# Sharing pooling and the gate's +1 with GpSimd, six gate groups by Sigmoid and a new instruction order in a pooled-attention and gated-convolution kernel

## The chip, the cores and the metric

The kernel runs on one core of a Trainium2 chip. The core has a matrix engine (TensorE, "PE" in the profile), three engines for element-wise work (VectorE "DVE", ScalarE "ACT", GpSimd "POOL") and SyncE "SP", which here only issues DMAs. Each engine executes its own instructions strictly in the order in which the program lists them, and waits on semaphores for the others. The metric is the device time of one execution in microseconds; the number quoted for a kernel is the median of its runs.

## The reference

Eight sequences of 576 rows are computed. For each, keys and values are averaged over groups of 8 rows, the 576 queries attend to the 72 pooled keys in 8 heads of 64, and the result goes through a feed-forward block in which a three-tap convolution along the sequence gates the hidden layer.

```python
k_p = k.reshape(B, H, Sp, pool, D).mean(axis=3)          # B, H, S, D = 8, 8, 576, 64; pool = 8
v_p = v.reshape(B, H, Sp, pool, D).mean(axis=3)
scores = scale * np.matmul(q, k_p.transpose(0, 1, 3, 2))
scores = scores - np.max(scores, axis=-1, keepdims=True)
attn = np.exp(scores)
attn = attn / (np.sum(attn, axis=-1, keepdims=True) + 1e-09)
x = np.matmul(attn, v_p)                                  # then heads side by side: (8, 576, 512)
h = np.maximum(x @ w_in, 0.0)                             # d_ff = 1024
conv_out = sum(conv_w[k] * hp[:, k:k + S, :] for k in range(3))   # hp is h, zero-padded by one row
gate = 1.0 / (1.0 + np.exp(-conv_out))
return h * gate @ w_out
```

Inputs and output are float32; inside, the matrices are bfloat16.

## The kernel before

**Groups and tiles.** The eight sequences ("b" 0 to 7) form four groups g of two. The 1152 rows of a group are cut into nine attention tiles t of 128 rows (ten in group 0, where the tile shared by both sequences is split in two of 64), 37 tiles in all. The rows of a sequence stand in an order in which row c of every run of nine lies together, so that a shift by one row is a shift by 64 columns with a wrap at the ends.

**Loads.** K of sequences 0 and 1, then K of the pairs (2,3), (4,5), (6,7), Q and V of each sequence, and the two weight matrices are loaded by DMAs that stand in POOL's queue (L272, L279, L290, L293, L300, L308). The load also converts to bfloat16. Buffers are few: one for a K pair (`kk`), four for Q (`qp`), three for V (`v`); a load into a buffer waits until the last use of what was in it.

**Pooling.** For sequences 0 and 1 K is pooled by a matmul with a pooling matrix (L391, L401). For the later pairs `pool_pair` (L424) adds halves in three steps on DVE, over all nine blocks at once: 128x2304, 128x1152 and 128x576 elements. V of every sequence is pooled by `prep_v`: three halving steps (L471, 128x1280, 128x640, 128x320) and a multiplication with a head mask into `vm` (L475, 128x960), all on DVE.

**Attention of a tile.** Scores (PE, L567 or L580), negated maximum (DVE, L593), the shift by it: either on DVE into a float32 tile `sd` (L605, 27 tiles) or as a matmul onto the scores (PE, L613, the ten tiles of group 0); exponential (ACT, L631); transposition of `e`, in groups 0 and 1 by PE and a copy (L642, L656), in groups 2 and 3 by a transposing DMA in SP's queue (L651); values with the sum of the exponentials in a 65th column (PE, L667); division (DVE, L680 and L682); transposition of `x`, again by PE and a copy (L699, L707) or by SP's DMA (L691).

**Feed-forward of a sequence.** For each of eight blocks fb of hidden columns 8 matmuls (L712) and a ReLU on ACT that writes 0.5·h (L721). Four blocks make a gate group f4, so there are 16 gate groups. In ten of them the convolution is done on PE with diagonal matrices (`ffn_conv`, L874), followed by Tanh on ACT (L899); half of the result comes out with its partition halves exchanged and goes to a side tile `tg`. In the other six (`TAPS`: (4,1), (5,0), (5,1), (6,0), (6,1), (7,0)) it is done by one ACT instruction (L847) and two DVE instructions (L849) for each block, then Tanh (L854). Since sigmoid(y) = (1 + tanh(y/2))/2, DVE then adds 1: L910 and two L912 (which undo the exchange) for a PE group, one L860 for a tap group. DVE multiplies by h (L920 or L861). The result is `gT`; 8 matmuls for each of 36 output tiles (L928), a copy (L939) and two stores (L951) follow. For sequences 4 to 7 POOL copies the wrapped ends of h (`ffn_wrap`, L796 and L797), which is POOL's only work beside loads and set-up.

**What sets the order.** Every piece of work is an `Op` in a `Graph`. The order of all instructions, the engine of those copies that DVE or ACT may do, and the buffer that each takes are written out in tables (`ORDER`, `FORMS`, `PLACES`); nothing is decided at run time. An entry -1 in `ORDER` stands for a filler matmul (L384) that computes nothing that is used.

Of the kernel before, what the change touches and what calls it, by code (L numbers as in the profile page):

```python
# [16 lines left out]

# [6 lines left out]
class Op:  # L24
    def __init__(self, engines, key, emit, uses, mode, land, count):
        self.engines, self.key, self.emit, self.mode, self.land, self.count = engines, key, emit, mode, land, count
        self.uses, self.next, self.left = list(uses), [], 0
        self.forms, self.like, self.dmas = None, None, 1
        self.ready, self.start, self.end, self.engine = 0.0, None, None, None
        for t in self.uses:  # L30
            t.users.append(self)


class Graph:

    SPARES = 150
    ATT = 90.28  # L40
    SPREAD = -122.92
    PREP_K = 135.88
    KPOOL = -99.86
    KTURN = 15.09
    PREP_Q = 1123.0
    PREP_V = 2242.18
    GATE = 390.96
    CONV = 199.25
    QCONV = -794.87
    OUT = 412.5  # L50
    LAST = 1107.48
    FIRST = 803.11
    V0 = -1430.11
    DW = -368.65
    X_DMA = 4
    APART = (0,)
    SIXTEEN = ()
    Q_DMA = (3,)
    WRAP = (4, 5, 6, 7)
    TAPS = ((4, 1), (5, 0), (5, 1), (6, 0), (6, 1), (7, 0))  # L60
    ACC = 2
    WRAPS = 2
    CROSS = ()
    BY_TILE = ()
    V_POOL = ()
    K_POOL = ()
    SHIFT_PE = ((0, 0), (0, 1), (0, 2), (0, 3), (0, 4), (0, 5), (0, 6), (0, 7), (0, 8), (0, 9))
    TURN_DMA = 2
    BANKS = 8
    ORDER = (  # L70
# [79 lines left out]
    def add(self, engines, key, emit, after=(), behind=(), uses=(), mode=None, land=None, count=10):  # L150
        o = Op(engines, key, emit, uses, mode, land, count)
        for a, started in [(x, False) for x in after] + [(x, True) for x in behind]:
            if a is not None:
                a.next.append((o, started))
                o.left += 1
# [22 lines left out]
def kernel(  # L178
# [13 lines left out]
    POOL = 8  # L192
# [59 lines left out]
    def buf(*key):  # L252
        return buffers[key[0]][tokens[key].slots[0]]
# [10 lines left out]
    def shift_by_dve(g, t):  # L264
        return (g, t) not in Graph.SHIFT_PE
# [1127 lines left out]
```

## Time and profile before

| | |
|---|---|
| runs | 222.36, 221.46, 221.68 us; median 221.68 |
| span of the profiled execution | 224.8 us |
| SP's transposing DMAs | 18 of `e`, 18 of `x`, 2 of Q |
| median time from issue to landing of a V load (512 KB) | 15.2 us |
| loads, software queue | 16.26 MB, 44.8% of 16 engines' span |
| HBM read and written | 32.52 MB, 9.44 MB |

The profile is of one execution, whose span from the first to the last instruction is longer by 3.1 us than the median of the runs. Busy time of PE is not PE at its peak, since matmuls are pipelined and their ends modelled. A row of a group gives the engine, the operation, what it writes and reads, the shape, the count, then busy microseconds and mean nanoseconds of one, then the idle time of the engine before them.

### The profile page before, as it was taken

The page shows a single profiled execution, that of the slowest core. Times are in us where ns is not written, and L with a number is a line of the kernel's source. Part 1 is how long each engine was busy: PE and PEld are TensorE (multiplying, and loading weights), DVE is VectorE, ACT ScalarE, POOL GpSimd, SP SyncE. Part 2 cuts the span into 40 slices and gives each one's busy share as a digit, 9 for nine tenths or more (in the row PEclk, how much of TensorE's full clock was granted, in tenths as well). Part 3 has the DMA queues.
Part 4 walks back from the last instruction along what each step waited for, and adds up shares of the span by engine and source line. Part 5 has one row for each costly group of instructions (what it writes and reads, how often), then busy time and mean ns, then how long its engine had stood idle before and what let it go on. Part 6 is the DMA issues. An engine that isn't in the chain of part 4 may idle for free.

```text
span 224.8 us, 6558 instructions
## 1 busy us (share of the span) xinstructions
PE 205.1 (91%) x2722; PEld 137.9 (61%) x2722; DVE 195.4 (87%) x337; ACT 160.9 (72%) x271; POOL 45.1 (20%) x81
## 2 busy tenths in 40 slices
PE   5897999979999999959999949989999999999991
PEld 1465778755788877636677735656656665654450
DVE  7889876999999999957999948999999999999641
ACT  2155768898999958844697935688889999997210
POOL 7943321131230120000000121001031230540000
PEclk9999999999999999988999988999999999999997
DMA  5999999999999999947664553168566617423495
GB/s 81 137 191 207 207 206 208 207 207 206 207 208 206 155 187 172 207 39 163 121 106 92 119 118 76 32 92 165 117 145 140 137 23 166 95 48 71 96 247 194
DMA packets 48833, 32.61 MB, mean 145 GB/s; under 512 B 28300, under 2 KB 44324, under 8 KB 48804
## 3 DMA queue, kind: packets, MB, share of 16 engines
q0 software_dynamic: 16288, 16.26, 44.8%
q1 hardware_dynamic: 31796, 14.96, 33.3%
q10 hardware_dynamic: 720, 0.98, 1.5%
q8 instruction: 21, 0.34, 0.6%
q14 instruction: 8, 0.07, 0.1%
HBM read 32.52 MB, written 9.44 MB: 187 GB/s over the span
## 4 chain that ended last, share of the span: by engine, by line
PE 44%; DVE 30%; DMA 8%; issue 7%; ACT 6%; POOL 3%; DVEq 0%; POOLq 0%
PE psum L928 21%; PE psum L712 14%; DVE negm L593 6%; DMA qp<-in_q_dram 6%; DVE x L682 5%; DVE sd L605 5%; PE psum L874 4%; DVE tg L849 2%; DVE gT L912 2%; PE psum L667 2%; DMA eT<-e 2%; DVE v L471 2%; DVE r L680 2%; DVE gT L920 2%; ACT e L631 1%
## 5 line engine op out<-in xcount | busy, mean ns | idle before, releaser
L712 PE MATMUL psum<-xT,w_in_sb 128*128 128x288 bf16 x512 | 74.4, 289 | 0.8 <-ACT tg L899 0.5
L928 PE MATMUL psum<-w_out_sb,gT 128*128 128x512 bf16 (+1 forms) x296 | 70.3, 378 | 0.5 <-DVE gT L920 0.5
L712 PEld LDWEIGHTS <-w_in_sb 128*128 128x128 bf16 x512 | 48.4, 99 | 17.6 <-issue 1.6
L721 ACT ACTIVATE hT<-psum 128x576 bf16<-128x576 f32 x64 | 40.1, 652 | 14.9 <-PE psum L712 14.3
L928 PEld LDWEIGHTS <-gT 128*128 128x128 bf16 x296 | 27.7, 98 | 27.0 <-issue 1.2
L849 DVE SCALAR_TENSOR_TENSOR tg<-hT,convw,tg 128x576 f32<-128x576 bf16 x48 | 37.3, 818 | 0.4
L593 DVE TENSOR_REDUCE negm<-psum 128x8 f32<-128x576 f32 (+2 forms) x37 | 27.4, 750 | 4.4 <-PE psum L567 3.9
L796 POOL COPY hT<-hT 128x126 bf16<-128x126 bf16 x16 | 9.1, 567 | 101.4 <-ACT hT L721 90.9
L682 DVE TENSOR_TENSOR x<-psum,r 128x512 bf16<-128x512 f32 (+1 forms) x37 | 25.6, 691 | 1.3
L667 PE MATMUL psum<-vm,eT 128*128 128x130 bf16 (+5 forms) x240 | 20.0, 227 | 4.1 <-DMA eT<-e 2.9
L874 PE MATMUL psum<-hT,dw 64*64 64x288 bf16 (+2 forms) x608 | 19.2, 261 | 2.6 <-issue 2.3
L667 PEld LDWEIGHTS <-eT 128*128 128x128 bf16 (+1 forms) x240 | 16.0, 103 | 9.1 <-DMA eT<-e 3.8
L605 DVE TENSOR_TENSOR sd<-psum,negm 128x576 f32<-128x576 f32 x27 | 20.1, 752 | 1.0 <-ACT e L631 0.5
L631 ACT ACTIVATE e<-sd 128x576 bf16<-128x576 f32 x27 | 18.6, 689 | 1.8 <-DVE sd L605 1.6
L874 PEld LDWEIGHTS <-dw 64*64 64x64 bf16 x608 | 14.8, 107 | 7.6 <-issue 6.7
L847 ACT ACTIVATE tg<-hT,convw 128x576 f32<-128x576 bf16 x24 | 18.0, 773 | 1.0 <-DVE gT L912 0.9
L899 ACT ACTIVATE tg<-psum 128x576 bf16<-128x576 f32 x20 | 13.0, 653 | 7.2 <-PE psum L874 7.2
L939 ACT COPY osb<-psum 128x512 f32<-128x512 f32 x25 | 14.5, 586 | 4.0 <-PE psum L928 3.9
L854 ACT ACTIVATE gT<-tg 128x576 bf16<-128x576 f32 x24 | 16.2, 685 | 0.8 <-DVE tg L849 0.3
L471 DVE TENSOR_TENSOR v<-v 128x1280 bf16<-128x1280 bf16 (+2 forms) x24 | 13.0, 540 | 2.1 <-DMA v<-in_v_dram 1.9
L899 ACT ACTIVATE gT<-psum 128x576 bf16<-128x576 f32 x20 | 12.9, 649 | 2.0 <-PE psum L874 2.0
L920 DVE TENSOR_TENSOR gT<-gT,hT 128x2304 bf16<-128x2304 bf16 x10 | 13.5, 1349 | 0.0
(82 smaller groups left out, 236.2 us busy)
## 6 DMA issues: line engine op xcount, KB each, us to landing
out_dram<-osb SPq DMA_DIRECT2D x54, 128.0 KB, 2.4
v<-in_v_dram POOLq DMA_DIRECT2D x8, 512.0 KB, 15.2
qp<-in_q_dram POOLq DMA_DIRECT2D x7, 576.0 KB, 16.9
kk<-in_k_dram POOLq DMA_DIRECT2D x3, 1152.0 KB, 17.6
out_dram<-qp SPq DMA_DIRECT2D x10, 128.0 KB, 2.9
w_in_sb<-in_moe_w_in_dram POOLq DMA_DIRECT2D x2, 512.0 KB, 17.3
w_out_sb<-in_moe_w_out_dram POOLq DMA_DIRECT2D x1, 1024.0 KB, 24.3
out_dram<-qp ACTq DMA_DIRECT2D x6, 128.0 KB, 2.7
```

Source lines behind the costliest of these rows:

```text
L593: nc.vector.tensor_reduce(out=a["m"][0:rows], in_=a["s"][0:rows, :, 0:2 * KW].rearrange("p a (h s) -> p a h s", s=Sp), axis=AX.X, op=OP.ma ...
L605: nc.vector.tensor_tensor(out=a["d"][0:rows], in0=a["s"][0:rows, :, 0:2 * KW].rearrange("p a (h s) -> p a h s", s=Sp), in1=a["m"][0:rows]. ...
L631: nc.scalar.activation(out=dst, in_=src, func=ACT.Exp, scale=1.0 / (POOL * 8.0),)
L667: nc.tensor.matmul(out=a["o"][lo:hi, h // 4, (h % 4) * (D + 1):(h % 4 + x1 - x0) * (D + 1)], lhsT=a["eT"][:, j, lo:hi], rhs=buf("vm", b)[: ...
L682: nc.vector.tensor_tensor(out=a["x"][0:rows].rearrange("p (a h d) -> p a h d", a=2, d=D), in0=ov[:, :, :, 0:D], in1=r[0:rows].unsqueeze(3) ...
L712: nc.tensor.matmul(out=banks(ps)[:, j, 0:SC], lhsT=w_in_block(dc, fb), rhs=buf("xT", g)[:, dc, i * S + j * SC:i * S + (j + 1) * SC], start ...
L721: nc.scalar.activation(out=h_of(b)[:, fb].rearrange("p (a s) -> p a s", a=2), in_=banks(ps)[:, :, 0:SC], func=ACT.Relu, scale=0.5,)
L847: nc.scalar.activation(out=acc, in_=h, func=ACT.Identity, scale=w)
L849: nc.vector.scalar_tensor_tensor(out=acc, in0=h, scalar=w, in1=acc, op0=OP.mult, op1=OP.add)
L874: nc.tensor.matmul(out=banks(pss[r ^ c])[c * D:(c + 1) * D, j, lo:hi], lhsT=dw[r * D:(r + 1) * D, tap * n_fb + fb, :], rhs=hT[r * D:(r + 1 ...
L899: nc.scalar.activation(out=t.rearrange("p (a s) -> p a s", a=2), in_=banks(ps)[:, :, 0:SC], func=ACT.Tanh, scale=0.5,)
L928: nc.tensor.matmul(out=bank(ps)[0:rows, columns], lhsT=buf("gT", g)[:, fb, t * P:t * P + rows], rhs=w_out_sb[:, fb, columns], start=(fb == 0),
```

## The change

- **Pooling in pieces, on either engine.** `pool_pair` and `prep_v` take a slice and an engine. A K pair is added in 3 + 2 + 1 pieces in place of three instructions, a V in 2 + 1 + 1 pieces and 2 for the mask in place of four. Of the 18 pieces for K 11 stand on POOL and 7 on DVE, of the 48 for V 25 on POOL and 23 on DVE.
- **The gate's +1 on either engine.** `raise_gate` adds 1, on POOL as a multiplication by 1 and an addition. The three instructions of a PE group and the two halves of a tap group are pieces of their own: 19 on POOL, 10 on DVE.
- **Sigmoid.** In the six groups (5,0), (5,1), (6,0), (6,1), (7,0), (7,1) ACT computes Sigmoid in place of Tanh, with ReLU scaled by 1 and not 0.5. The five tap groups among them then need no +1; (7,1) still needs two copies to undo the exchange. Sigmoid takes a second table load on ACT, and the order keeps every exponential ahead of every Sigmoid.
- **ReLU on either engine.** Eight of 64 ReLUs stand on DVE (L710 of the changed kernel).
- **Transposes.** The choice between PE and DMA is made tile by tile: `e` of 22 tiles (four of group 1 besides all of groups 2 and 3), `x` of 24 tiles (six of group 1 besides) go by DMA. The shift goes by PE in 13 tiles (seven of group 0, five of group 1, one of group 3).
- **Convolution.** `ffn_conv` reads wrapped ends only in the tap groups; all ten PE groups use the 64-matmul form, where the four convolutions of (4,0) and (7,1) used 48. POOL's wrap copies fall from 16 pairs to 12.
- **Copies and stores.** DVE copies five `eT` (two before) and eight `xT` (four before); 21 stores are issued from ACT (nine before). Some clears move from DVE to POOL.
- **Order.** All tables are new. One filler stands in the order in place of 22. The pooling matrix and other early data lie in `gT` buffer 0 in place of 1.

```diff
+    CHOICE = {
+        "shift": {
+            (0, 0): 1, (0, 1): 1, (0, 2): 1, (0, 3): 1, (0, 4): 1, (0, 7): 1, (0, 8): 1, (1, 2): 1, (1, 3): 1, (1, 5): 1,
+            (1, 6): 1, (1, 7): 1, (3, 3): 1,
+        },
...
+        "sigma": {
+            (5, 0): 1, (5, 1): 1, (6, 0): 1, (6, 1): 1, (7, 0): 1, (7, 1): 1,
+        },
+    }
...
-    def pool_pair(g, step):
-        t, half = buf("kk", g), POOL * D >> step + 1
-        engine = nc.gpsimd if g in Graph.K_POOL else nc.vector
+    def pool_pair(g, step, cs, engine):
+        t, half = buf("kk", g)[:, cs], POOL * D >> step + 1
         engine.tensor_tensor(out=t[:, :, 0:half], in0=t[:, :, 0:half], in1=t[:, :, half:2 * half], op=OP.add)
...
+    def ffn_relu(b, fb, ps, o):
+        out = h_of(b)[:, fb].rearrange("p (a s) -> p a s", a=2)
+        scale = 1.0 if graph.chosen("sigma", b, fb // 4) else 0.5
+        if o.engine == "DVE":
+            nc.vector.tensor_scalar(
+                out=out, in0=banks(ps)[:, :, 0:SC], scalar1=scale, scalar2=0.0, op0=OP.mult, op1=OP.max
+            )
+            return
+        nc.scalar.activation(out=out, in_=banks(ps)[:, :, 0:SC], func=ACT.Relu, scale=scale)
...
+    def gate_func(b, fb):
+        return ACT.Sigmoid if graph.chosen("sigma", b, fb // 4) else ACT.Tanh
+
+    def raise_gate(engine, b, fb, out, in_):
+        if graph.chosen("sigma", b, fb // 4):
+            engine.tensor_copy(out=out, in_=in_)
+        elif engine is nc.gpsimd:
+            engine.tensor_scalar(out=out, in0=in_, scalar1=1.0, scalar2=1.0, op0=OP.mult, op1=OP.add)
+        else:
+            engine.tensor_scalar(out=out, in0=in_, scalar1=1.0, scalar2=None, op0=OP.add)
...
+        for step, cuts in ((0, (0, 3, 6, 9)), (1, (0, 5, 9)), (2, (0, 9))):
+            now = []
+            for lo, hi in zip(cuts, cuts[1:]):
+                cs = slice(lo, hi)
+                before = [o for o, x in steps if x.start < hi and lo < x.stop]
+                o = add(fast(1, (hi - lo) * (POOL * D >> step + 1)), None, after=before or [loads["kk", g]], uses=[kk[g]])
+                then(o, lambda o, step=step, cs=cs: pool_pair(g, step, cs, hand(o)))
+                now.append((o, cs))
+            steps = now
...
+        steps = [(lv[b], slice(0, NJ))]
+        for step, cuts in enumerate(((0, 3, 5), (0, 5), (0, 5), (0, 3, 5))):
...
+    for o in sigmas:
+        for e in exps:
+            graph.follow(e, o)
```

More of the change, by code (lines that the diff above doesn't have):

```diff
@@ L985, with add_load @@
-    seq = [START]
-    def nudge(kind, b):
-        return 0.0
-    def soon():
-        seq[0] += 0.01
-        return seq[0]
-    loads = {}
-    kk, kp, qp, qTt = {}, {}, {}, {}
-    kb = B and H * S * D * 4
-    def add_load(kind, b, key, share=1.0, **part):
+    n_outs = {b: [t for t in range(9) if (t < 4) == (i == 0)] for b, (g, i) in where.items()}
+    kb = H * S * D * 4
+    loads, kp, qp, qTt = {}, {}, {}, {}
+    kk0 = token("kk", 0)
+    kk = {0: kk0}
+    def add_load(kind, b, share=1.0, **part):
@@ L1047 @@
-    hmw = add(dve(1.15), soon(), widen_mask, after=[hm])
-    dw0 = add({"DVE": 0.3}, soon(), lambda: build_conv_matrices(0, cwtok), after=[cwp], uses=[cwtok])
-    dwo = [add({"DVE": 1.0}, START + Graph.DW + n, lambda n=n: build_conv_matrices(n), after=[dw0]) for n in (1, 2)]
-    win = [add({"POOL": 0.74}, first("w%d" % j), lambda j=j: load_w_in(j), land=(LATE, 2 * P * d_ff * 4, RATE)) for j in range(2)]
-    wout = add({"POOL": 0.9}, first("out"), load_w_out, land=(LATE, d_ff * d_model * 4, RATE))
@@ L1053, in add_load_pair @@
+    def add_load_pair(g):
         kk[g] = token("kk", g)
[L1054 to L1057 removed]
+        loads["kk", g] = add({"POOL": 1.03}, lambda: load_pair(g), uses=[kk[g]], land=(1.3, 2 * kb, 1))
+    for b in range(1, B):
         if b == 1:
[L1059 to L1063 removed]
@@ L1159 @@
-    xtok, xdone = {}, {}
+        steps = [(lv[b], slice(0, NJ))]
+        for step, cuts in enumerate(((0, 3, 5), (0, 5), (0, 5), (0, 3, 5))):
+            now = []
+            for lo, hi in zip(cuts, cuts[1:]):
+                js = slice(lo, hi)
+                o = add(fast(1, (hi - lo) * (POOL * D >> step + 1 if step < 3 else 3 * D)), None,
+                        after=[o for o, x in steps if x.start < hi and lo < x.stop] + ([hmc, hmw] if step == 3 else []),
+                        uses=[vtok[b]] + [vmtok[b]] * (step == 3))
+                then(o, lambda o, step=step, js=js: prep_v(b, step, js, hand(o)))
+                now.append((o, js))
+            steps = now
@@ new lines, in add_out, with queue @@
+            then(o, lambda o, t=t, sm=sm: ffn_copy(g, t, sm, copier(o)))
+            o = add({"SP": 1.3, "ACT": 1.16}, None, after=[o], uses=[osb], land=(2.4, 0, 1))
+            then(o, lambda o, t=t: ffn_store(g, t, queue(o)))
+    def queue(o):
+        return nc.scalar if o.engine == "ACT" else nc.sync
+    for b in range(B):
+        if b < 2:
+            add_prep_k(b)
+        elif b % 2 == 0:
+            add_pair(b // 2)
+        add_prep_q(b)
+        add_prep_v(b)
+    for b in range(B):
+        for t in n_tiles[b]:
+            add_att(where[b][0], t)
```

704 lines of the change are left out of this document (292 added, 412 removed), and 123 rows, old and new, of tables (CHOICE, ORDER, PLACES).

## The prediction

> **What bounds the kernel now.** I read the sums of the page first, then the busy time of each engine by stretches, then what ended the two holes that these show.
>
> ```profile
> span 224.8 us, 6558 instructions
> PE 205.1 (91%) x2722; PEld 137.9 (61%) x2722; DVE 195.4 (87%) x337; ACT 160.9 (72%) x271; POOL 45.1 (20%) x81
> ```
>
> ```profile
> core 0: us, PE busy (x) PEld busy (x) DVE busy (x) ACT busy (x) POOL busy (x), PEclk, DMA share, GB/s
> 40.00:90.00 50.00, 47.73 (x813) 36.21 (x802) 49.01 (x87) 44.32 (x77) 8.81 (x12) 1.00 1.20 195
> 90.00:110.00 20.00, 17.56 (x280) 11.57 (x275) 15.64 (x27) 11.41 (x19) 0.00 (x0) 0.91 0.80 134
> 110.00:130.00 20.00, 19.83 (x356) 14.99 (x354) 19.43 (x35) 17.11 (x30) 1.01 (x2) 1.00 0.56 107
> 130.00:140.00 10.00, 7.12 (x73) 4.45 (x72) 6.09 (x10) 3.70 (x8) 2.31 (x6) 0.83 0.48 100
> 140.00:210.00 70.00, 69.09 (x600) 41.67 (x599) 68.14 (x98) 60.58 (x101) 13.77 (x24) 1.00 0.49 103
> ```
>
> PE looks busiest, but its ends are modelled. What it needs can be had from the last stretch of output matmuls, where nothing else is in its way:
>
> ```profile
> 206.60 13.21 PE L928 MATMUL psum<-w_out_sb,gT 128*128 128x512 bf16 x68
> L712 PE MATMUL psum<-xT,w_in_sb 128*128 128x288 bf16 x512 | 74.4, 289 | 0.8 <-ACT tg L899 0.5
> L928 PE MATMUL psum<-w_out_sb,gT 128*128 128x512 bf16 x280 | 68.5, 385 | 0.5 <-DVE gT L920 0.5
> ```
>
> The 68 are 52 of 512 and 16 of 256 columns, 30,720 columns in 13.21 us, or 0.43 ns each. At that rate the 512 and 280 dense matmuls need 63.5 + 61.7 = 125 us, where the rows have 142.9. PE's busy 205 us thus holds some 18 us of waiting, and 187 us is the most that its work can need. DVE has no such slack: in 40 to 90, 110 to 130 and 140 to 210 it is busy 136.6 of 140 us. These 140 us are DVE's. The other two middle stretches are holes: DVE idles 4.4 us in 90 to 110 and 3.9 us in 130 to 140. Their causes in the order of time:
>
> ```profile
> 85.62 8.64 SPq L513 DMA_TRANSPOSE qT<-qp  x1
> 94.44 7.85 SPq L651 DMA_TRANSPOSE eT<-e  x2
> 98.30 0.53 PE L874 MATMUL psum<-hT,dw 64*64 64x288 bf16 x13 [2.29 <-issue]
> 102.38 2.02 SPq L513 DMA_TRANSPOSE qT<-qp  x1
> 133.56 0.84 PE L667 MATMUL psum<-vm,eT 128*128 128x130 bf16 x6 [2.88 <-DMA eT<-e]
> ```
>
> The same kind of transposing DMA held SP for 8.64 us at 85.62 and for 2.02 us at 102.38. The last V load was issued at 82.96 (row below) and takes 15.2 us to land, so the first fell among loads and the second behind them. At the end of the two slow ones PE stood 2.29 us without a wait that the profile can name. The second hole is a late `eT`, with no load in flight.
>
> **The change, part by part.** DVE is the stage bound, so DVE's sum comes first.
>
> ```profile
> L910 DVE TENSOR_SCALAR gT<-gT 128x1152 bf16<-128x1152 bf16 x10 | 5.3, 530 | 0.0
> L912 DVE TENSOR_SCALAR gT<-tg 64x1152 bf16<-64x1152 bf16 x20 | 9.1, 455 | 0.3
> L860 DVE TENSOR_SCALAR gT<-gT 128x2304 bf16<-128x2304 bf16 x6 | 4.8, 800 | 0.1
> L471 DVE TENSOR_TENSOR v<-v 128x1280 bf16<-128x1280 bf16 x8 | 6.5, 818 | 1.9 <-DMA v<-in_v_dram 1.9
> L471 DVE TENSOR_TENSOR v<-v 128x640 bf16<-128x640 bf16 x8 | 3.9, 485 | 0.1
> L471 DVE TENSOR_TENSOR v<-v 128x320 bf16<-128x320 bf16 x8 | 2.5, 318 | 0.1
> L475 DVE TENSOR_TENSOR vm<-v,mask_wide 128x960 bf16<-128x960 bf16 x8 | 5.2, 651 | 0.1
> L424 DVE TENSOR_TENSOR kk<-kk 128x2304 bf16<-128x2304 bf16 (+2 forms) x9 | 7.7, 853 | 0.1
> L605 DVE TENSOR_TENSOR sd<-psum,negm 128x576 f32<-128x576 f32 x27 | 20.1, 752 | 1.0 <-ACT e L631 0.5
> ```
>
> *The +1.* 19.2 us go; eight 64-row pieces and two 128-row pieces stay: 8 x 0.455 + 2 x 0.530 = 4.7. Gain 14.5. *V.* From 1280 and 640 elements, 0.52 ns an element and 0.15 us fixed. 18.1 us go. DVE keeps two pieces of 768 (0.55), four of 512 (0.42), four of 640, five of 320, and for the mask five of 576 (0.45) and three of 384 (0.35): 9.6 us. Gain 8.5. *K.* 7.7 us go, five pieces of 768, one of 640 and one of 512 stay: 3.7. Gain 4.0. *Shift.* 27 become 24: 2.3. Together 29.3.
>
> ```profile
> L656 DVE COPY eT<-psum 128x640 bf16<-128x640 bf16 x1 | 0.5, 480 | 0.0
> L707 DVE COPY xT<-psum 128x512 bf16<-128x512 bf16 x4 | 1.5, 418 | 0.0
> L721 ACT ACTIVATE hT<-psum 128x576 bf16<-128x576 f32 x64 | 40.1, 652 | 14.9 <-PE psum L712 14.3
> L1036 ACT ACT_TABLE_LOAD x1 | 1.3, 1283 | 0.8 <-PEq L1377 0.8
> ```
>
> DVE takes on eight ReLUs. No row shows one on DVE; the nearest, L605, also reads 576 float32 from psum and takes 0.752: 6.0 us (with 0.48, the copy of 640, as the lower bound 3.8; with 0.818, the V step of 1280, 6.5). Three more `eT` and four more `xT` copies: 1.4 + 1.7 = 3.1. **DVE's own sum: -29.3 + 6.0 + 3.1 = -20.2 us.** ACT loses eight ReLUs (5.2 us) and gains a table load (1.3) and 12 store issues; it was idle 9.4 of 70 us in the DVE-bound stretch, so the load's 1.3 is all I charge. The Trainium skill, "ScalarE: Activation LUTs", section "What ACT_TABLE_LOAD costs", gives about 2.66 us for a switch of set with its drain, where this row has 1.283; by it the sum would be 1.4 us higher.
>
> *What POOL takes.* Its work in this trace, and how it meets DVE:
>
> ```profile
> 138.85 1.42 DVE L593 TENSOR_REDUCE negm<-psum 128x8 f32<-128x576 f32 x2 [0.65 <-PE psum L567]
> 138.95 0.30 POOL L796 COPY hT<-hT 128x126 bf16<-128x126 bf16 x1
> 139.19 0.30 POOL L797 COPY hT<-hT 128x126 bf16<-128x126 bf16 x1
> 200.97 0.81 POOL L797 COPY hT<-hT 128x126 bf16<-128x126 bf16 x1
> 198.60 5.51 DVE L849 SCALAR_TENSOR_TENSOR tg<-hT,convw,tg 128x576 f32<-128x576 bf16 x7
> L849 DVE SCALAR_TENSOR_TENSOR tg<-hT,convw,tg x48: 800/814/892, 130.4 to 204.2; 128x576 f32<-128x576 bf16 x48
> L316 POOL TENSOR_SCALAR_AFFINE_SELECT gT<-gT 64x648 bf16<-64x648 bf16 x2 | 1.6, 796 | 0.1
> ```
>
> The same copy takes 0.30 us at 139, while DVE takes maxima out of psum, and 0.81 us at 201, among taps that read two tiles of SBUF: about the length of one tap. So POOL waits for such a DVE instruction to finish. The other way round these copies cost DVE next to nothing: no tap took over 892 ns against a median of 814, and seven with copies among them took 5.51. But 126 elements are short, and the new pieces have 320 to 1152. L316 gives 1.23 ns an element for one input. I take that per input: 21 gate pieces of 1152 make 30 us, and the pooling pieces (7,104 elements for K, 13,824 for V, two inputs) 51 us; 81 us in 57 pieces, 1.42 us each. POOL has the time (45 of 225 us are used). What it costs DVE: some 50 DVE instructions outside the taps read two SBUF tiles or are fast copies (30 pooling pieces, ten +1, ten products). If POOL holds them whenever it is at work, 81 us in the 158 before the last 67 (see the first rival) meet each with 0.51, for half a piece: 50 x 0.51 x 0.71 = 18 us. The lower bound is 0, as the taps show; a gain is excluded. These pieces lie nearer in length to the taps than to the copies, so neither end is near, and I take the middle, **+10 us**.
>
> That upper end is also what the Trainium skill says in "SBUF — State Buffer", section "SBUF: two separate sides": whichever of the two starts first has the shared port pair for its whole instruction and the other blocks. The trace agrees for POOL waiting (0.81 for 0.30); that DVE waits as long is shown by no row here. By that rule the term would be 18 and the sum 8 us higher.
>
> *Transposes.* Ten tiles of group 1 go from PE and a copy to SP (four `e`, six `x`), and the new order is meant to keep them out of the loads. The first hole is worth 4.4, the second, not of that cause, 3.9. A better order could win both (-8), a transposing DMA that still meets loads costs a hole of 4 each (two: +8). I take -3. *Fillers and the second clock.* The 22 fillers ran in idle time; without them PE may run slower after a pause, as in 130 to 140, where the clock is 0.83: 1.7 us for ten. I take +1, from 0 to 3. PE loses 10 transposition sets and gains three shifts; it is not the bound, so nothing.
>
> Sum on the profiled execution: 224.8 - 20.2 + 1.3 + 10 - 3 + 1 = 213.9 us. The median of the runs, 221.68, is 3.1 below its span; **211 us**.
>
> **The rivals.** *POOL's queue makes the last loads late (slower).* Loads stand in POOL's queue behind pieces now.
>
> ```profile
> 46.07 1.03 POOL L279 DMA_DIRECT2D kk<-in_k_dram  x1 [3.88 <-DVE r L680]
> 82.96 0.77 POOL L290 DMA_DIRECT2D v<-in_v_dram  x1 [6.66 <-DVE vm L475]
> v<-in_v_dram POOLq DMA_DIRECT2D x8, 512.0 KB, 15.2
> L631 ACT ACTIVATE e<-sd x27: 672/686/717, 51.2 to 169.1; 128x576 bf16<-128x576 f32 x27
> ```
>
> Between K of the third pair (46.07 now) and the last V (82.96 now) come 33 pieces: 48 us at the rate above, and 3 for a fixed part (the copies of 126 elements follow each other at 0.24 us, 0.085 over the rate). Issues of 0.77 to 1.03 add some 7. That puts the last V at 104 us, no harm. If each piece first waits for a DVE instruction as long as a V step (0.82), add 27, and if the seven that follow a DVE piece find it 0.75 late, 5: 136. Then 15 us to land, and 11 us for the last sequence's five tiles (three DVE instructions of 0.75 each). In the program 77 ACT instructions stand behind the last exponential, 64 before; today 55.7 us follow its start, so 67 will, because no Sigmoid may come earlier. 136 + 15 + 11 + 67 = 229, less 3.1: **226 us**. It decides once the last V is issued after 132. For it: POOL is in order and no row shows a two-input operation on it. Against: 28 us of slack.
>
> *DVE's gain is eaten (no gain).* Collisions at 18 us and no hole won: 224.8 - 20.2 + 1.3 + 18 + 1 = 224.9, less 3.1: **222 us**; with one hole won 218. This is also the case in which the change does not do what it says: nothing in SP's queue waits for a load to end, so transposes can meet loads that run late.
>
> *DVE is fully relieved (faster still).* No collisions and both holes gone: 224.8 - 20.2 + 1.3 - 8.3 = 197.6; there PE's need (187, less the fillers, plus start and tail) would decide at about 205 of span: **202 us**.
>
> **How the numbers follow.** Forecast 0.50, late loads 0.22, gain eaten 0.16, full relief 0.12. The forecast's own range is 204 to 219 (collisions 3 to 18; the rivals lie beyond). The range reaches to full relief below and just past the late loads above: 203 to 227, with about 0.07 left out below and 0.11 above. Within 0.5% (1.1 us, what a measurement of this kernel can tell from no change) I put 0.06, all from the middle of the eaten gain. Faster: 0.50 + 0.12 + 0.06 of the eaten gain (one hole won) = 0.68; slower: 0.22 + 0.04 = 0.26.
>
> **What would show it.** DVE busy near 175 to 185 us instead of 195; products and pooling pieces on DVE longer than the rows above by up to one POOL piece if it is held (right at 10 us in sum); POOL at 120 to 130 us busy; no SP transposition over 3 us while loads run; the last V issued before 115. Wrong: DVE still above 190 busy or idle in new holes of 5 us behind `kk`, `v` or `eT`; the end of the exponentials later than 150; PE idle over 20 us between 40 and 200.

## The result, and the profile after

| | median us | runs |
|---|---|---|
| changed kernel | 238.65 | 239.3, 238.75, 238.55, 235.29 |
| kernel before, same session | 221.57 | 222.36, 221.46, 221.68, 219.08 |

The ratio is 1.073, with a 95% interval of 1.063 to 1.083: the change makes the kernel 17 us slower. 211 us were forecast, within 203 to 227. In what follows a ratio always stands against runs of the kernel before on the same chip in the same session. Ratios leave disturbed runs out and medians do not (one run of e4 took 492 us and one of e13 1113 us), so comparisons between sessions go by ratios, where 1% is 2.2 us, and a difference of two medians is only a rough size.

The sums of the page, changed kernel:

```profile
span 237.2 us, 6858 instructions
PE 202.6 (85%) x2823; PEld 138.3 (58%) x2841; DVE 188.6 (79%) x300; ACT 149.6 (63%) x249; POOL 121.7 (51%) x140
```

DVE's work did fall, by 6.8 us, and POOL is as busy as forecast. But DVE's idle time rose from 29.4 to 48.6 us, and PE's from 19.7 to 34.6. (In every other run the time is 1.7 to 2.1 us above the span of its profile, so the execution profiled before, with a span of 224.8, took some 226.7 us, an estimate, 5 more than the median; the rise in idle time is if anything larger than these figures.) The same stretches as in the prediction, changed kernel (busy us of PE, weight loads, DVE, ACT, POOL; clock, DMA share, GB/s):

```profile
core 0: us, PE busy (x) PEld busy (x) DVE busy (x) ACT busy (x) POOL busy (x), PEclk, DMA share, GB/s
40.00:90.00 50.00, 43.06 (x846) 34.11 (x845) 43.36 (x75) 32.02 (x55) 37.07 (x37) 0.97 1.03 159
90.00:110.00 20.00, 13.47 (x252) 8.18 (x253) 13.12 (x16) 9.71 (x16) 12.87 (x10) 0.87 1.10 172
110.00:130.00 20.00, 16.79 (x191) 10.38 (x193) 15.03 (x24) 6.46 (x11) 15.88 (x13) 0.96 0.74 119
130.00:140.00 10.00, 9.71 (x202) 7.77 (x205) 5.49 (x9) 8.61 (x15) 5.78 (x5) 1.00 0.69 156
140.00:210.00 70.00, 67.23 (x719) 44.60 (x729) 67.56 (x97) 58.33 (x96) 27.73 (x37) 1.00 0.56 104
```

From 40 to 130 us no engine is full any more. DVE, which was busy 49 of 50 us in the first of these stretches, is busy 43, and in 90 to 110 only 13 of 20. From 140 on PE and DVE are nearly as full as before. What was late can be seen in two pieces of the chain that ended last (start, duration, what):

```profile
72.64 7.18 DMA xT<-x
94.47 9.84 DMA eT<-e
```

and in the timeline (start, duration, engine, line, operation; in brackets the idle time before and what ended it):

```profile
79.86 0.66 PE L698 MATMUL psum<-xT,w_in_sb 128*128 128x288 bf16 x4 [2.45 <-DMA xT<-x]
104.38 0.68 ACT L617 ACTIVATE e<-sd 128x576 bf16<-128x576 f32 x1 [7.82 <-DMA eT<-e]
105.66 2.01 PE L839 MATMUL psum<-hT,dw 64*64 64x288 bf16 x29 [4.84 <-ACT gT L854]
108.21 0.76 DVE L579 TENSOR_REDUCE negm<-psum 128x8 f32<-128x576 f32 x1 [6.09 <-PE psum L553]
```

A transposing DMA issued at 94.47 lands 9.84 us later. Until then it holds its `e` buffer, and the exponential that wants this buffer waits 7.82 us. Behind that exponential stand the Tanh of a gate, and behind the Tanh TensorE's convolution (4.84 us) and VectorE's maximum (6.09 us). How much later the transposes land is in the list of DMA issues (count, median us from issue to landing), first of the kernel before, then of the changed one:

```profile
eT<-e SPq DMA_TRANSPOSE x18, 2.6
xT<-x SPq DMA_TRANSPOSE x18, 2.4
```

```profile
xT<-x SPq DMA_TRANSPOSE x24, 3.1
eT<-e SPq DMA_TRANSPOSE x22, 3.7
qT<-qp SPq DMA_TRANSPOSE x2, 7.7
```

The median of `e` rises from 2.6 to 3.7 us, and the two of Q take 7.7. Taken one by one, 1 of the 31 transposing DMAs whose landing is recorded lands more than 6 us after its issue in the kernel before, and 8 of 41 in the changed one. Five of the eight are issued between 94 and 121 us, while loads that left between 78 and 94 us, or at 118.36 and 119.18, are on their way; in the kernel before the last load left at 83.72. No wait of an engine after 38 us in the changed kernel is put down to a load itself: those that a DMA ended were ended by a transposition or by a store.

VectorE's own groups (busy us, mean ns), changed kernel:

```profile
L816 DVE SCALAR_TENSOR_TENSOR tg<-hT,convw,tg 128x576 f32<-128x576 bf16 x48 | 40.2, 877 | 0.8
L873 DVE TENSOR_TENSOR gT<-gT,hT 128x2304 bf16<-128x2304 bf16 x16 | 25.3, 1592 | 0.3
L668 DVE TENSOR_TENSOR x<-psum,r 128x512 bf16<-128x512 f32 x35 | 24.2, 691 | 1.2
L788 DVE TENSOR_SCALAR gT<-tg 64x1152 bf16<-64x1152 bf16 x8 | 6.2, 770 | 0.2
L710 DVE TENSOR_SCALAR hT<-psum 128x576 bf16<-128x576 f32 x8 | 6.0, 754 | 3.5 <-PE psum L698 3.4
L411 DVE TENSOR_TENSOR kk<-kk 128x768 bf16<-128x768 bf16 x5 | 4.6, 939 | 0.0
```

Taps, products, the 64-row +1 and the pooling pieces for K have become longer (818, 1349, 455 ns and an estimate of 550 before); the division, which reads psum, has not (691).

### The profile page after: what moved, and what is told of

It is laid out like the page before. It is cut to its first block, busy times and chain, and to the rows that moved or that the text cites. A ratio compares the mean times of both kernels' runs of the same rounds, so it can differ in the third digit from the quotient of the medians.

```text
span 237.2 us, 6858 instructions
## 1 busy us (share of the span) xinstructions
PE 202.6 (85%) x2823; PEld 138.3 (58%) x2841; DVE 188.6 (79%) x300; ACT 149.6 (63%) x249; POOL 121.7 (51%) x140
## 4 chain that ended last, share of the span: by engine, by line
PE 53%; DVE 14%; DMA 12%; ACT 7%; POOL 6%; issue 5%; ACTq 1%; DVEq 0%; POOLq 0%
PE psum L881 18%; PE psum L698 18%; PE psum L839 6%; DMA eT<-e 5%; PE psum L653 3%; DVE x L668 3%; DVE negm L579 3%; DMA xT<-x 3%; DMA qp<-in_q_dram 3%; POOL v L457 2%; PE psum L628 2%; POOL gT L786 1%; ACT gT L854 1%; DMA out_dram<-osb 1%; DVE sd L591 1%
## 5 line engine op out<-in xcount | busy, mean ns | idle before, releaser
L881 PE MATMUL psum<-w_out_sb,gT 128*128 128x512 bf16 (+1 forms) x278 | 65.9, 379 | 1.4 <-issue 0.7
L714 ACT ACTIVATE hT<-psum 128x576 bf16<-128x576 f32 x56 | 35.4, 649 | 16.6 <-PE psum L698 15.9
L579 DVE TENSOR_REDUCE negm<-psum 128x8 f32<-128x576 f32 (+3 forms) x37 | 27.4, 752 | 13.8 <-PE psum L553 11.5
L873 DVE TENSOR_TENSOR gT<-gT,hT 128x2304 bf16<-128x2304 bf16 x16 | 25.3, 1592 | 0.3
L457 POOL TENSOR_TENSOR v<-v 128x768 bf16<-128x768 bf16 (+3 forms) x17 | 24.6, 1454 | 0.6
L617 ACT ACTIVATE e<-sd 128x576 bf16<-128x576 f32 (+1 forms) x24 | 16.2, 682 | 11.1 <-DMA eT<-e 8.0
L653 PE MATMUL psum<-vm,eT 128*128 128x65 bf16 (+5 forms) x240 | 19.8, 227 | 2.5 <-DVE eT L642 1.4
L786 POOL TENSOR_SCALAR gT<-tg 64x1152 bf16<-64x1152 bf16 x10 | 11.8, 1178 | 19.0 <-ACT tg L854 18.6
L814 ACT ACTIVATE tg<-hT,convw 128x576 f32<-128x576 bf16 x24 | 17.7, 767 | 2.0 <-DVE gT L788 1.9
L591 DVE TENSOR_TENSOR sd<-psum,negm 128x576 f32<-128x576 f32 (+1 forms) x24 | 17.9, 754 | 1.0
L411 POOL TENSOR_TENSOR kk<-kk 128x768 bf16<-128x768 bf16 (+3 forms) x11 | 17.2, 1563 | 2.9 <-DVE kk L411 2.5
```

The source lines that it names most:

```text
L457: engine.tensor_tensor(out=vt[:, :, 0:half], in0=vt[:, :, 0:half], in1=vt[:, :, half:2 * half], op=OP.add)
L579: nc.vector.tensor_reduce(out=a["m"][0:rows], in_=a["s"][0:rows, :, 0:2 * KW].rearrange("p a (h s) -> p a h s", s=Sp), axis=AX.X, op=OP.ma ...
L591: nc.vector.tensor_tensor(out=a["d"][0:rows], in0=a["s"][0:rows, :, 0:2 * KW].rearrange("p a (h s) -> p a h s", s=Sp), in1=a["m"][0:rows]. ...
L653: nc.tensor.matmul(out=a["o"][lo:hi, h // 4, (h % 4) * (D + 1):(h % 4 + x1 - x0) * (D + 1)], lhsT=a["eT"][:, j, lo:hi], rhs=buf("vm", b)[: ...
L714: nc.scalar.activation(out=out, in_=banks(ps)[:, :, 0:SC], func=ACT.Relu, scale=scale)
L814: nc.scalar.activation(out=acc, in_=h, func=ACT.Identity, scale=w)
```

## The experiments

Theories at the start: A, the loads come late out of POOL's queue; B, the ten transposes of group 1 by DMA are in each other's and the loads' way; C, POOL's pieces collide with DVE and hold up the chain; D, the start is late. The first four kernels each undo one thing in the changed kernel (238.65 us, ratio 1.073).

**e1: group 1's ten transposes by TensorE and ScalarE again.**

```diff
-            o.emit()
...
+            if o.tag in BY_PE:
...
+                (att_turn if kind == "send" else att_turn_out)(g, t, ps)
...
+            for copy, g, t in late.get(p, ()):
+                copy(g, t, nc.scalar.copy)
```

> Undoes one part: the ten group-1 transposes go through TensorE and a ScalarE copy again; all else is the changed kernel. Theory B (the group-1 transposes stand in SP's queue among loads and hold e, eT and xT): the 21.8 us of SP at 74 and the holes at 74-86 and 97-110 go, 225 to 230 us. Theory A (the loads come late out of POOL's queue and the burst from 72.6 us is what hurts): qT and the first transposes of group 2 stay in the burst, so only part comes back, 231 to 236 us. Theory C (POOL's pieces slow DVE and hold up the chain): 237 to 240 us, as the changed kernel's 238.65. DVE busy stays near 188 under all three.

**e2: all 57 pieces on VectorE** (each entry of `ORDER` with POOL's parity takes DVE's: 165 becomes 164, and so on).

> Undoes one part: all 57 pieces of pooling and +1 on GpSimd go back to VectorE at the same places of the order. Theory C (collisions and POOL's slow pieces): DVE busy rises from 188.6 by the pieces' own sum (about 20) less the collisions (about 13), so to 194 to 198, taps back to 818 ns and 64-row +1 to 455 ns, and the time falls to 228 to 233 us because nothing waits in POOL's queue. Theory A: the loads come out early too (last V load before 100 us), 228 to 233 us as well; what tells them apart is loads_early. Theory B: SP's long transposes stay, DVE has more to do, 240 to 246 us.

**e3: four loads earlier in POOL's queue.** Pairs of the load's entry and the entry ahead of which it goes:

```diff
+    MOVES = ((52, 72), (88, 196), (80, 222), (86, 211))
```

> Changes the place of four loads in POOL's queue alone: w_out and q7 at once behind kk2 and q5, v5 and v6 ahead of kk2's pooling pieces (about 66 us in place of 72.6 and 79.2). Theory A: the idle DMA time of 55-72 us is filled, the burst is over about 15 us earlier, SP's 21.8 us falls under 8, 228 to 233 us. Theory B: the collisions only move to the transposes of 59-72 us, 236 to 242 us. Theory C: 237 to 240 us.

**e4: the rest of q0 earlier.**

```diff
+    MOVES = ((34, 12),)
```

> Moves one load: the rest of q0 directly behind k0 in POOL's queue, ahead of the pooling matrix and the mask. Theory D (the start is 3.6 us late because of that load's place): first maxima at about 12.5 us in place of 15.1 and 235 to 237 us. If the start is hidden by the waits on loads at 72-110, the first maxima come earlier and the time stays at 238 to 239 us.

| | median us | ratio | 95% |
|---|---|---|---|
| e1 | 239.17 | 1.086 | 1.076 to 1.096 |
| e2 | 253.29 | 1.146 | 1.142 to 1.151 |
| e3 | 242.97 | 1.099 | 1.089 to 1.109 |
| e4 | 236.89 | 1.071 | 1.064 to 1.077 |

None recovered the loss; e4's 1.8 us are within the intervals. e2 says that this order needs the sharing: without it VectorE is busy 199.5 us and the time is longer by 7.3% of the kernel before, 16 us. e3 sent the loads earlier and 11 of 41 transposes then landed late. In e1 the holes at 79 and 104 us are gone, but new ones stand at 50 to 80 us, where in-order engines wait for one another, partly for copies at places that I chose and the order was not made for. Nor does e1 part transposes from loads: 6 of its 34 recorded landings take more than 6 us, one transposed Q 21.96. The stretches 50 to 80 and 80 to 110 us, first the changed kernel, then e1:

```profile
core 0: us, PE busy (x) PEld busy (x) DVE busy (x) ACT busy (x) POOL busy (x), PEclk, DMA share, GB/s
50.00:80.00 30.00, 24.61 (x535) 19.48 (x532) 26.90 (x50) 20.23 (x34) 25.19 (x28) 1.00 0.90 128
80.00:110.00 30.00, 23.47 (x368) 15.95 (x370) 20.21 (x25) 14.08 (x23) 17.92 (x14) 0.86 1.14 183
```

```profile
50.00:80.00 30.00, 23.29 (x411) 17.89 (x408) 19.00 (x38) 19.40 (x32) 18.43 (x21) 0.89 0.43 70
80.00:110.00 30.00, 25.72 (x471) 18.35 (x473) 23.86 (x33) 19.82 (x34) 21.86 (x20) 1.00 1.23 178
```

DVE gains 3.7 us in the second stretch and loses 7.9 in the first. So an edit that moves work in an order written by hand has a price of its own, and a test of the DMAs has to leave the order alone. I sharpened B into theory T (a transposing DMA lands late while loads move, and what waits for its buffers makes the holes), against theory O (the new order makes the engines wait for one another whatever the DMAs do).

**e5: the loads after 50 us cut, order and instructions unchanged.**

```diff
+        heads = slice(0, 1) if b > 4 else heads
...
+        cs = slice(0, 2 if g > 1 else C)
...
-        vt = buf("v", b)
+        vt, n = buf("v", b), 1 if b > 4 else 4
```

> The changed kernel, but the loads of q, k and v issued after 50 us move only a part of their bytes (q a quarter, k two ninths, v a quarter of its large part); the rest is left out and the old contents of the buffers are computed on. Order, queues, instructions and their places are the same. Theory T (transposing DMAs are held while loads move, and what waits for them makes the holes): SP's 21.8 us and 7.4 us fall under 3 us, the holes at 74-86 and 97-110 go, 222 to 229 us. Theory O (the new order makes the engines wait for one another whatever the DMAs do): 233 to 238 us. Between the two (229 to 233) both have a part.

**e6: e1 with earlier loads** (`MOVES` of five loads: w_out and q7 behind q5, v5 and v6 ahead of kk2's pieces, kk3 behind kk2's turn).

> Group 1's ten transposes by TensorE and ScalarE copies as in e1, and five loads earlier in POOL's queue (w_out and q7 behind q5, v5 and v6 ahead of kk2's pooling pieces, kk3 behind kk2's turn). Theory T: each of e1 and e3 alone only moved the meeting of loads and transposes; both together part them, so DMA has no gap at 55-72 us, SP has no row over 10 us before 110 us, and the time is 226 to 232 us. Theory O: 237 to 243 us, as e1 and e3.

**e7: the old order with the ten transposes by DMA.**

```diff
+            moved = g == 1 and t in (0, 1, 4, 5)
-            o = add(pe(*[rows] * 5), key, lambda: att_turn(g, t, sm), after=[o, ze], uses=[sm, e, eT],
+            o = add(pe(*[rows] * 5), key, lambda: att_send(g, t) if moved else att_turn(g, t, sm), after=[o, ze], uses=[sm, e, eT],
...
+            sent = g == 1 and t in (0, 1, 2, 3, 7, 8)
```

> The kernel before with one part of the change alone: the same ten group-1 transposes go by DMA at the places of its TensorE transposes, their copies fall away. Theory T: the loads of the old order run without a break to 65 us and on to 90, the ten meet them, SP stands over 25 us in rows over 3 us, and the time is 230 to 250 us. If transposing DMAs cost what they cost between loads (1.2 us), TensorE and the copies are relieved by 2.4 and some 5 us and the time is 218 to 223 us.

**e8: the old order with one piece of the +1 of each gate group on GpSimd.**

```diff
+        nc.gpsimd.tensor_scalar(out=gate[D:2 * D, 1], in0=tg[0:D], scalar1=1.0, scalar2=1.0, op0=OP.mult, op1=OP.add)
         nc.vector.tensor_scalar(out=gate[:, 0], in0=gate[:, 0], scalar1=1.0, scalar2=None, op0=OP.add)
```

> The kernel before with one part of the change alone: in each of the 16 gate groups one piece of the +1 (64x1152 or 128x1152) goes to GpSimd, beside VectorE's own pieces. VectorE's own sum falls by 10 x 0.455 + 6 x 0.35 = 6.7 us. If collisions eat it (theory C) VectorE's busy time falls by less than 2 us and the time is 222 to 226 us; if a third is eaten, VectorE's busy time falls by 4 to 5 us and the time is 219 to 222 us, little of it because TensorE has 9.4 to 9.9 us of real columns in each 10 us from 160 us on.

| | median us | ratio | 95% | transposes landing after more than 6 us |
|---|---|---|---|---|
| e5 | 226.12 | 1.021 | 1.012 to 1.030 | 0 of 41 |
| e6 | 238.29 | 1.076 | 1.068 to 1.084 | 3 of 34 |
| e7 | 240.10 | 1.085 | 1.078 to 1.093 | 7 of 43 |
| e8 | 228.43 | 1.034 | 1.025 to 1.044 | |

e5 and e7 are the two that decide. With the loads cut the changed kernel gets back 5.2% by the ratios (11.5 us; 12.5 by the medians) without any instruction being moved. With the ten transposes alone the old order becomes 18.5 us slower, though TensorE and the copies have less to do. In the chain of e7 two transposing DMAs take 25 us:

```profile
65.90 15.82 DMA xT<-x
95.51 9.17 DMA eT<-e
```

and engines wait for late transposes directly, VectorE for an `x` buffer that one of them holds:

```profile
73.24 0.83 PE L667 MATMUL psum<-vm,eT 128*128 128x130 bf16 x6 [5.63 <-DMA eT<-e]
81.82 0.69 DVE L682 TENSOR_TENSOR x<-psum,r 128x512 bf16<-128x512 f32 x1 [4.28 <-DMA xT<-x]
104.72 0.84 PE L667 MATMUL psum<-vm,eT 128*128 128x130 bf16 x6 [5.95 <-DMA eT<-e]
```

These three make 15.9 us. What e7 would cost with the loads cut was not tried, so how much of its 18.5 us is the new places of the work and not the loads stays open.

One number in my expectations was misread. SP's row at 74 us in the timeline of the changed kernel:

```profile
74.01 21.79 SPq L637 DMA_TRANSPOSE eT<-e  x3
```

The same row of e5:

```profile
72.56 19.23 SPq L639 DMA_TRANSPOSE eT<-e  x3
```

And SP's waits for exponentials in the changed kernel (us in total, times, longest):

```profile
SPq L637 <- ACT e L617: 73.4, 4, 58.2
```

The 21.79 us are three issues with waits between them: beside the long first wait there are 15.2 us in three others. So the expected fall of this row under 3 us could not come; the landing is what changes. e6 is inconclusive: three late landings only, but it carries e1's new waits (DVE busy 17.7 of 30 us in 50 to 80).

In e8 VectorE has 6.7 us less to do and is busy 197.6 us in place of 195.4. The timeline shows how:

```profile
122.11 1.15 POOL L911 TENSOR_SCALAR gT<-tg 64x1152 bf16<-64x1152 bf16 x1 [16.16 <-ACT tg L900]
122.99 0.58 DVE L912 TENSOR_SCALAR gT<-gT 128x1152 bf16<-128x1152 bf16 x1
125.42 1.15 POOL L911 TENSOR_SCALAR gT<-tg 64x1152 bf16<-64x1152 bf16 x1 [2.16 <-ACT tg L900]
125.87 1.01 DVE L912 TENSOR_SCALAR gT<-gT 128x1152 bf16<-128x1152 bf16 x1
126.91 0.46 DVE L913 TENSOR_SCALAR gT<-tg 64x1152 bf16<-64x1152 bf16 x1
```

VectorE's +1 takes 0.45 us by itself. Here it starts 0.88 and 0.45 us into GpSimd's piece and ends 0.31 us behind the piece's end both times: it stood still until GpSimd was done. A group that hands one piece over and does the other two meanwhile gains nothing.

**e9: only the six late transposes by TensorE** (e1 without the four that are issued before 70 us).

> The changed kernel with only those six of group 1's ten transposes by TensorE and ScalarE copies that it issues from 70 us on (turns of tiles 0 and 1, outputs of tiles 8, 7, 0 and 1); the four before stay DMAs. Theory T (a transposing DMA lands after 7 to 10 us where loads move and 2.5 us where not, and each late one holds a buffer): ScalarE's 7.8 us and TensorE's 4.8 us at 104 us and the 2.45 us at 79 us go, 229 to 233 us. If the copies on ScalarE and the waits on TensorE take back what that brings, as in e1, 236 to 240 us.

**e10: the 21 pieces of the +1 on VectorE; e11: the 36 pooling pieces on VectorE** (parity of their entries, as e2).

> The changed kernel with its 21 pieces of the +1 and of the gates' copies on GpSimd given back to VectorE at the same places; the 36 pooling pieces stay on GpSimd. By e8 (16 such pieces on GpSimd made the old order 6.9 us slower): 230 to 235 us, VectorE's busy time no higher than 190. If this order needs them on GpSimd, as e2 has it for all 57: 243 to 248 us, VectorE's busy time 193 to 196.

> The other half of e2: the 36 pooling pieces of k and v go back to VectorE, the 21 pieces of +1 stay on GpSimd. If the two halves add up, e10 and e11 together differ from the changed kernel by the 14.6 us of e2: 249 to 256 us where e10 is faster than the changed kernel, 240 to 246 us where e10 is slower. Theory A (pooling in POOL's queue makes the loads late): 230 to 236 us.

**e12: the old order with the loads cut** as in e5.

> The kernel before, with the loads after 46 us cut to the same parts as in e5 (k of groups 2 and 3, q and v of sequences 5 to 7); the rest is left out. It shows what the meeting of loads with transposes costs the old order, where the first transposing DMA stands at 80 us. Theory T: little, 217 to 221 us, so that of the 17 us between the two kernels some 8 to 12 are this. If the old order gains as much as the changed one (12.5 us), 208 to 212 us, the loads hold both kernels alike and are not what tells them apart.

| | median us | ratio | 95% |
|---|---|---|---|
| e9 | 235.17 | 1.051 | 1.039 to 1.062 |
| e10 | 240.38 | 1.070 | 1.059 to 1.080 |
| e11 | 245.13 | 1.102 | 1.091 to 1.111 |
| e12 | 218.79 | 0.985 | 0.977 to 0.992 |

e12 is the control for e5: by the ratios the old order gains 1.6% or 3.4 us from the cut, the changed one 5.2% or 11.5 us. **About half of the loss, 8 of 16 us, is the meeting of transposes with loads**, with some 3.5 us either way from the three intervals; the medians give 9.9 of 17. The granted clock of the changed kernel rises with the cut too, from 0.978 to 0.996 (at 90 to 110 us, where TensorE stood, from 0.87 to 1.00); what that is worth was not separated. e9 is faster than the changed kernel by 2.2% or 3.5 us of the medians, less than expected, and 8 of its 39 recorded landings are still late: it shows that the six transposes cost something at their places, not that parting them from the loads helps. e10 cannot be told from the changed kernel: in the new order the shared +1 brings nothing that these runs can tell. e11 shows that the shared pooling does (2.9%).

**e13: Sigmoid alone on the old order** (the five groups behind its last exponential). **e14: pooling pieces alone on the old order.**

```diff
+        if (b, f4) not in SIGMA:
+            nc.vector.tensor_scalar(out=gate, in0=gate, scalar1=1.0, scalar2=None, op0=OP.add)
...
+        if step == 0 and b > 1:
+            pool_part(vt[:, 3:5], POOL * D // 2, nc.gpsimd)
+            pool_part(vt[:, 0:3], POOL * D // 2, nc.vector)
```

> The kernel before with one part of the change alone: Sigmoid in the five gate groups whose gates stand behind the last exponential of the old order ((5,0), (6,0), (6,1), (7,0), (7,1)). VectorE's own sum falls by 4 x 0.80 + 0.45 = 3.7 us, ScalarE gets one table load (1.3 us). Since TensorE has 9.4 to 9.9 us of real columns in each 10 us from 160 us on, I expect 220 to 222 us, the kernel before or up to 1.5 us faster; if VectorE set the pace there, 218 us.

> The kernel before with one part of the change alone: 15 pooling pieces on GpSimd (for v of sequences 2 to 7 two of the five blocks of the first step and of the spread, for k of groups 1 to 3 a third of the first step) at the old places. VectorE's own sum falls by 6 x (0.31 + 0.26) + 3 x 0.45 = 4.8 us. If collisions eat it and the pieces hold up the loads behind them, as the +1 pieces of e8 did: 224 to 230 us. If pooling shares well (e11 has the 36 pooling pieces worth 6.5 us in the new order): 217 to 221 us.

**e15: e5 with all 57 pieces on VectorE. e16: e5 with the old start** (`MOVES` of q0's load and of the memset for the fillers, and 22 fillers).

> e5 (loads after 50 us cut, rest left out) with all 57 pieces back on VectorE. If sharing with GpSimd costs what is left of the 17 us: 217 to 222 us, as the old order with small loads (218.8). If the order needs the sharing: 234 to 242 us, as e2 against the changed kernel (+14.6); then the order or the start is what costs the rest.

> e5 with the old start: q0's second load directly behind k0, and 22 filler matmuls between TensorE's first steps. If the start costs the 2 to 5 us by which TensorE's real columns are behind at 60 us: first maxima at 11.5 to 12.5 us, 221.5 to 224 us. If the start is swallowed later: 225 to 227 us.

**e17: e5 with POOL's 36 pooling pieces cut to an eighth; e18: the same with the loads whole.**

```diff
+        n = half // 8 if engine is nc.gpsimd else half
-        engine.tensor_tensor(out=t[:, :, 0:half], in0=t[:, :, 0:half], in1=t[:, :, half:2 * half], op=OP.add)
+        engine.tensor_tensor(out=t[:, :, 0:n], in0=t[:, :, 0:n], in1=t[:, :, half:half + n], op=OP.add)
```

> e5 (loads after 50 us cut) with the 36 pooling pieces on GpSimd cut to an eighth of their columns as well (the rest of the pooling is left out; the buffers of vm are cleared at the start). GpSimd is relieved of about 40 us, its collisions with VectorE fall by some two thirds; VectorE's own instructions are the same. If GpSimd's queue and the collisions cost the rest of the difference: 216 to 220 us. If the order of the engines among themselves costs it: 224 to 227 us.

> The changed kernel with the 36 pooling pieces on GpSimd cut to an eighth of their columns and the loads whole. If GpSimd's in-order queue makes the loads late (rival R1 of the prediction): the loads of 72 to 80 us are issued 5 us or more earlier, fewer transposes land later than 6 us, and the time is 224 to 231 us. If the loads' places in the order set their time: issue times within 3 us of the changed kernel's, 235 to 239 us.

| | median us | ratio | 95% |
|---|---|---|---|
| e13 | 224.46 | 1.008 | 1.003 to 1.012 |
| e14 | 224.53 | 1.017 | 1.012 to 1.022 |
| e15 | 249.87 | 1.125 | 1.117 to 1.133 |
| e16 | 227.60 | 1.033 | 1.029 to 1.037 |
| e17 | 225.55 | 1.024 | 1.018 to 1.029 |
| e18 | 237.87 | none computed | |

On the old order none of the four parts is a gain by itself in the form tried: transposes 8.5%, the +1 3.4%, pooling 1.7% (1.2 to 2.2) slower, and Sigmoid 0.8% (0.3 to 1.2), too little to call more than no gain. Why Sigmoid gains nothing was not followed up. e15 shows that with cut loads too the new order depends on the sharing (23 us by the ratios). e16 acquits the missing fillers, but not the start: its first maximum comes at 14.22 us, as in e5 (14.27), where the old order has it at 11.59 (e12), so its edit did not bring the old start back. e17 acquits POOL's queue with cut loads: with most of its pooling time gone (POOL busy 82 us in place of 119) the time stays. With whole loads (e18, POOL busy 83 us in place of 122) the four runs spread from 233.49 to 243.98 us, too far to exclude a gain of a few us. In e18 the loads of 72 to 80 us leave 3 to 4 us earlier, the last V load at 116.62 in place of 118.36, and six transposes still land late. With whole loads no version beat the kernel before.

What the other half is (3.6% or 8 us by the ratios, 226.12 against 218.79 by the medians, both with cut loads) is argued from rows and was not tried; the start, 2.7 us later, may be part of it. Output matmuls alone, by stretches, in e12 (old order) and e5 (new order):

```profile
core 0: us, PE busy (x) PEld busy (x), PEclk, DMA share, GB/s
30.00:60.00 30.00, 6.17 (x24) 2.05 (x24) 1.00 1.21 202
60.00:90.00 30.00, 2.05 (x8) 0.74 (x8) 1.00 0.49 89
```

```profile
core 0: us, PE busy (x) PEld busy (x), PEclk, DMA share, GB/s
30.00:60.00 30.00, 0.00 (x0) 0.00 (x0) 1.00 0.99 164
60.00:90.00 30.00, 2.40 (x12) 1.09 (x12) 1.00 0.77 102
```

The old order has 8.2 us of output matmuls done by 90 us, the new one 2.4. The 5.8 us have to be done later; that they are what makes the end late is not shown. A test would be an order that differs in this alone; none was made.

## Why the prediction was wrong, step by step

- **Where the sum missed.** On the profiled spans 213.9 us were forecast and 237.2 measured. Of the 23.3 us only 3.4 are DVE's busy time (185.2 forecast, 188.6 measured); 20 are its idle time (28.7 forecast, 48.6 measured). So the step that failed lies in the holes.
- **DVE's own sum, -20.2 us: right to within some 2 us.** I sorted VectorE's instructions by whether a POOL instruction was at work beside them. Taps 814 ns alone and 993 beside (17 of 48), products 1354 and 1777 (9 of 16), the 64-row +1 454 and 876 (6 of 8), `kk` pieces 551 and 1036 (4 of 5), one piece of `vm` 0.87 and one of V 0.82 us longer. The excess is 3.0 + 3.8 + 2.5 + 1.9 + 0.9 + 0.8, before rounding 13.0 us. Without it DVE would be busy 188.6 - 13.0 = 175.6; the prediction gives 195.4 - 20.2 = 175.2. The ReLU on DVE takes 754 ns (0.752 taken).
- **Collisions, +10: right in mechanism, too small by 3.** I left the taps out, and they carry 3.0. The rule of the Trainium skill that I weighed ("SBUF — State Buffer", "SBUF: two separate sides") lets the one that starts first block the other for its whole instruction, where VectorE's instruction is in a two-port mode or has two inputs in SBUF. The trace agrees. From 30 us on, of VectorE's instructions with all operands in SBUF, all 27 that started while a GpSimd instruction was under way became longer, by 0.03 to 1.18 us, and 14 of the 15 beside which GpSimd started second did not. Instructions that read psum were not held: the division takes 692 ns alone and 691 beside. So the taps of the kernel before, which the prediction took for a lower bound of 0, are not exempt: the nine that met a copy under way had only 0.23 to 0.29 us of it left.
- **Transposes and holes, -3 (from -8 to +8): the step that failed, with the wrong sign.** The meeting of transposes with loads measured some +8 on the new order (e5 against e12, by the ratios; 9.9 by the medians), and the ten transposes +18.5 on the old one (e7, places included). Two errors made it. I priced a meeting by how long SP's queue stood (8.64 us of "held"), where the price is the time from issue to landing, during which the buffers stay taken: from 130 us on, behind the last load, a median of 2.6 us and at most 4.7 in the changed kernel, among loads up to 9.84 there and 15.82 in e7. And I took the sign from "the new order is meant to keep them out of the loads", which is a purpose and not a row. The lines were misread as well: the row of 7.85 us at 94.44 is two issues of 1.2 us with a wait between, landed after 3.9 and 2.6 us, and the 15.2 us given to the last V load are the median of eight loads, where that one landed after 11.2. And the holes to be won were those of one long execution: in e8, with the old order, DVE is busy 19.36 of the 20 us from 90 to 110. My sentence under the second rival, that nothing in SP's queue waits for a load to end, was the right mechanism; I gave it 0.16 and no price. The rest of the loss, another 8 us by e5 against e12, stays open.
- **The sum in DVE's time taken as the sum in the kernel's time: failed too.** "These 140 us are DVE's" held for the old order only. In e17, with cut loads and 37 us less work on POOL, DVE is busy 184.3 us and the kernel takes as long as with 186.3 in e5; the old order with cut loads is faster with 194.3. Where an order leaves DVE waiting, work taken from DVE buys nothing.
- **Fillers, +1 (0 to 3): nothing against it** (e16: putting them back gains nothing).
- **Late loads (0.22, 226 us): the mechanism did not decide.** The last V load left at 118.36 (104 forecast, 132 needed), and relieving POOL's queue changed nothing with cut loads (e17); with whole ones the loads left 3.7 us earlier and six transposes still landed late (e18). But where the loads stand matters: behind the load of 118.36 the transposes of 119.2 and 120.6 took 7.31 and 6.52 us to land. **Full relief (0.12): refuted.**
- **What was to show it.** POOL busy 121.7 (120 to 130, right); DVE 188.6 (175 to 185 right, above 190 wrong: in between, by the collisions); holes of 5 us behind `eT`: there, at 104 us; last V before 115: missed; no SP transposition over 3 us among loads: missed, one of Q held SP for 7.42 us at 97.20; the last exponential later than 150: there, at 172.6 us (169.1 before); PE idle over 20 us from 40 to 200: just not, 19.6. The range ended at 227, since the transposes' upper bound was two holes of 4 us.

## What to carry to other kernels

Price a DMA by its time from issue to landing in the company of what else moves then, and by who waits for the buffers that it holds; the time for which its queue stands tells neither. A sum of an engine's saved time becomes the kernel's time only where the new order still keeps that engine full, so check what fills it stretch by stretch. Hand a piece to GpSimd beside VectorE work that reads psum, or let VectorE's own instruction start first, and put one part of a change alone on the old order first: here one experiment each shows that none of four parts pays in the form tried.

## What the runs showed of the hardware that was not expected

- Ten transposing DMAs among loads cost 18.5 us on an order in which they take work off two engines (e7); one of them took 15.82 us to land, where the medians of the kernel before are 2.4 and 2.6.
- VectorE waits for the end of a GpSimd instruction that is already under way when its own operands lie in SBUF alone (27 of 27 in the changed kernel; +1 of 128x1152: 0.45 us alone, 1.01 beside), and hardly ever when it starts first (1 of 15), so that 6.7 us less of its own work left VectorE busy 2.2 us longer (e8).
- A GpSimd piece of 64x1152 takes 1178 ns and one of 128x1152 1193: half the partitions save nothing.

```profile
L786 POOL TENSOR_SCALAR gT<-tg 64x1152 bf16<-64x1152 bf16 x10 | 11.8, 1178 | 19.0 <-ACT tg L854 18.6
L786 POOL TENSOR_SCALAR gT<-gT 128x1152 bf16<-128x1152 bf16 x9 | 10.7, 1193 | 5.4 <-ACT gT L854 5.3
```
